# Loading the second chunk of x in halves, moving a weight load ahead of two others, and a new instruction order, in a fused adaLN / linear-attention / SwiGLU kernel

## The chip, the cores and the metric

The kernel runs on one core of a Trainium2 chip. The metric is the device time of one execution in microseconds (us). The kernel before takes about 215 us: 216.03 in the three runs that the prediction had, and medians of 214.80 to 215.99 in the jobs of this study. Executions are compared in the same state. All medians and verdicts below are of fast executions; where a profile fell in the slow state I say so.

## The reference

One transformer block on x of 2048 rows by 512, with modulation from a vector c (`w_mod` gives six vectors of 512):

```python
sa, ca, ga, sb, cb, gb = split(silu(c) @ w_mod)          # six vectors of 512
h = layernorm(x) * (1 + ca) + sa
q, k, v = split(h @ wqkv)                                 # 32 heads of 16
phi = lambda t: concat(softmax(t @ w_phi), softmax(-(t @ w_phi)))   # per head
kv, z = phi(k).T @ v, sum(phi(k))                         # over all 2048 rows
o = (phi(q) @ kv) / (phi(q) @ z + 1e-6)
x = x + ga * (o @ wo)
h = layernorm(x) * (1 + cb) + sb
x = x + gb * ((silu(h @ w_gate) * (h @ w_up)) @ w_down)   # width 1376
```

What matters for the argument: the sum over all rows (`kv`) must be complete before the first attention product can start. The program therefore has a first stage (all keys and values, with the query projections beside it), a hand-over, and a second stage (attention, output projection, feed-forward).

## The kernel before

The program is a list of operations, each with an engine, a planned duration and buffers. A list `ORDER` (one number for an operation, four times its index plus the choice of engine) fixes how they follow each other on each engine. `QUOTA` limits how many PSUM banks each kind of product holds. TensorE therefore works strictly in the listed order: a product that waits for a load stops everything behind it.

All large loads go through SyncE's DMA queue, in this order; `later` and `transposed` put a DMA further back in the same queue:

```python
at_x[0, 0] = load(nc.sync, x_ch[0][:, 0:2, :], ...)       # x in 4 chunks of 512 rows
at_wk = [load(...), load(...)]                             # key weights
at_m1 = [load(nc.sync, wmod_sb[:, k, 0:2 * D], ...) for k in range(KD)]
at_x[0, 1] = load(...)
at_wv = load(...)                                          # value weights
at_x[1] = load(nc.sync, x_ch[1][:], x_v[1], 512)
at_wq = load(nc.sync, wqkv_sb[:, :, 0:D], ...)             # query weights
at_x[2] = load(...)
at_x[3] = load(...)
...
fold_phi(0, Wq2, bWq2, bwq)        # 4 DMA transposes (WT) of the query weights, then 4 products with w_phi
later(wmod_sb[:, :, 2 * D:6 * D], wmod_v[:, :, 2 * D:6 * D])      # second part of w_mod, 2 MB
```

`fold_phi` multiplies the query weights by w_phi once, so that the query projection needs no second product. It needs the weights transposed; for the query weights this is done by DMA, one slice of 128 rows at a time (`WT`).

One tile of 128 rows takes this path in the first stage: a key product (TensorE), two exponentials (ScalarE, `e`), a row sum and a reciprocal (VectorE, `S`, `R`), the product `phik = e * R` (GpSimd, 1.93 us), a copy of the values (`va`), and eight small key-value products of 65 columns that accumulate in PSUM. Four VectorE operations (`KVZ`) read the accumulators at the hand-over.

Fillers are products on a tile of ones, put into planned gaps of TensorE to keep its clock up:

```python
n, each = (4 * (P - HG - 1), 0.108) if not early and not late else (CW, 0.216)
...
fns += [f] * int((o.start - t0 - 0.1) * FILL / each)      # FILL = 0.85 of the gap
```

The softmax here doesn't subtract the row's maximum and nothing guards it: scores larger than these inputs give would overflow.

## Time and profile before

| view of the profile before | value |
|---|---|
| time, median of 3 | 216.03 us |
| span of the profiled execution | 213.2 us |
| TensorE busy | 200.7 us, 94% |
| second part of w_mod: issued, landed | 19.14, 27.32 us |
| TensorE's wait for it | 1.73 us at 27.4 |
| last `phik` on GpSimd ends | 58.6 us |
| first attention product | 61.50 us |

The busy time of TensorE contains fillers, so this document uses the measure that the prediction works out below. **Lag** at a point of the program is the clock time minus the useful product time issued so far. Lag grows when TensorE waits, runs a filler, or runs at half clock. It stays flat where TensorE never waits. Because the useful work is the same in all kernels here, the lags of two kernels at the same useful work say directly which is ahead.

### The profile page before, as it was taken

Reading aid. Unit: us, or ns where it says so; the run is one execution under the profiler, and the core shown is the slowest. Engines: PE = TensorE matmul, PEld = TensorE weight load, DVE = VectorE, ACT = ScalarE, POOL = GpSimd, SP = SyncE. Lnnn points to the kernel's source line nnn. Section 1 sums busy time; section 2 is a strip of 40 time slices with the busy share of each in tenths; the row PEclk is TensorE's granted clock in tenths of the full one; section 3 lists DMA queues with packets and bytes.
Section 4 is the critical chain, followed back from the end, with each engine's and each line's share of the span. In section 5 each row is a group of like instructions: output and inputs, shape, how many; then the busy total and the mean of one; then the engine's idle time right before and its main releaser. Section 6 shows DMA issues by size and latency. Waiting matters only on the chain.

```text
span 213.2 us, 4730 instructions
## 1 busy us (share of the span) xinstructions
PE 200.7 (94%) x1779; PEld 140.2 (66%) x1807; DVE 149.8 (70%) x352; ACT 118.9 (56%) x241; POOL 115.7 (54%) x157
## 2 busy tenths in 40 slices
PE   4997789999999999998999999999999999999993
PEld 1853554555555687786867877777776687777772
DVE  5799969999686977677887596677577764532314
ACT  2677989998889873433533603443342465363230
POOL 5257998899920535672642743654584563441340
PEclk9999999999999999999999999999999999999998
DMA  6996970389600011312221121123211222010001
GB/s 195 363 350 104 389 84 20 71 285 402 217 3 0 0 28 29 74 38 39 54 49 49 39 64 31 46 51 74 52 25 49 51 50 51 28 25 26 28 25 49
DMA packets 30793, 19.24 MB, mean 90 GB/s; under 512 B 22481, under 2 KB 28082, under 8 KB 30770
## 3 DMA queue, kind: packets, MB, share of 16 engines
q1 hardware_dynamic: 30480, 18.85, 31.8%
q8 instruction: 14, 0.23, 0.5%
q10 hardware_dynamic: 290, 0.08, 0.2%
q14 instruction: 9, 0.07, 0.1%
HBM read 11.58 MB, written 2.10 MB: 64 GB/s over the span
## 4 chain that ended last, share of the span: by engine, by line
PE 77%; DMA 13%; SPq 3%; DVE 3%; issue 1%; POOL 1%; DVEq 0%; POOLq 0%
PE one_ps L869 31%; PE one_ps L904 16%; PE one_ps L642 6%; PE one_ps L817 6%; PE one_ps L590 5%; PE one_ps L586 5%; DMA wmod_sb<-in_w_mod_dram 4%; DMA wqkv_sb<-in_A_wqkv_dram 4%; PE four_ps L746 3%; SPq L318 2%; DMA raw<-xn 2%; DMA oT<-o 2%; PE kv_ps L618 2%; DMA wphi_sb<-in_A_w_phi_dram 2%; DVE x_c L820 1%
## 5 line engine op out<-in xcount | busy, mean ns | idle before, releaser
L876 ACT ACTIVATE sg<-one_ps 128x512 bf16<-128x512 f32 (+3 forms) x52 | 27.2, 529 | 44.3 <-PE one_ps L869 39.8
L869 PE MATMUL one_ps<-hT,wu_sb 128*128 128x256 bf16 (+3 forms) x440 | 45.7, 251 | 0.8 <-DVE hT L840 0.8
L869 PE MATMUL one_ps<-hT,wg_sb 128*128 128x256 bf16 (+3 forms) x440 | 44.5, 251 | 0.0
L904 PE MATMUL one_ps<-wd_sb,gu 128*128 128x512 bf16 (+3 forms) x172 | 42.0, 366 | 0.8
L869 PEld LDWEIGHTS <-wu_sb 128*128 128x128 bf16 (+1 forms) x440 | 36.9, 100 | 8.8 <-issue 0.9
L869 PEld LDWEIGHTS <-wg_sb 128*128 128x128 bf16 (+1 forms) x440 | 36.9, 100 | 7.7
L885 POOL TENSOR_TENSOR gu<-usb,sg 128x512 bf16<-128x512 bf16 (+1 forms) x22 | 22.6, 1026 | 22.8 <-ACT sg L876 15.8
L611 POOL TENSOR_TENSOR phik<-e,R 128x1024 bf16<-128x1024 bf16 x16 | 30.6, 1930 | 3.5 <-DVE R L609 2.2
L879 DVE TENSOR_TENSOR gu<-one_ps,sg 128x512 bf16<-128x512 f32 (+2 forms) x30 | 17.8, 595 | 15.9 <-PE one_ps L869 13.0
L904 PEld LDWEIGHTS <-gu 128*128 128x128 bf16 (+1 forms) x187 | 17.8, 98 | 11.9
L375 DVE BATCH_NORM_STATS2 st<-x_c 128x6 f32<-128x512 bf16 x32 | 21.2, 680 | 1.7 <-DMA x_c<-in_A_x_dram 1.4
L883 ACT CAST usb<-one_ps 128x512 bf16<-128x512 f32 (+1 forms) x22 | 11.3, 525 | 18.8 <-PE one_ps L869 15.8
L911 DVE TENSOR_TENSOR fg<-one_ps,gab 128x512 bf16<-128x512 f32 (+1 forms) x17 | 11.2, 656 | 14.8 <-PE one_ps L904 14.5
L804 POOL TENSOR_TENSOR o<-o 128x512 bf16<-128x512 bf16 x14 | 16.2, 1157 | 8.7 <-DVE o L784 8.7
L607 DVE TENSOR_REDUCE S<-e 128x64 f32<-128x1024 bf16 x16 | 19.0, 1194 | 2.2 <-ACT e L597 2.1
L784 DVE TENSOR_TENSOR o<-four_ps,A 128x512 bf16<-128x512 f32 x32 | 20.6, 684 | 0.0
L915 POOL TENSOR_TENSOR ot<-x_c,fg 128x512 bf16<-128x512 bf16 x8 | 9.2, 1154 | 18.5 <-DVE fg L911 18.5
L597 ACT ACTIVATE e<-one_ps 128x512 bf16<-128x512 f32 x32 | 17.3, 607 | 2.7 <-PE one_ps L586 1.7
L648 ACT ACTIVATE eT<-one_ps 128x512 bf16<-128x512 f32 x32 | 17.5, 644 | 1.2 <-PE one_ps L642 1.1
L817 PE MATMUL one_ps<-wo_sb,oT 128*128 128x512 bf16 x60 | 16.2, 379 | 0.5 <-DMA oT<-o 0.3
L820 DVE TENSOR_TENSOR x_c<-x_c,one_ps 128x512 bf16<-128x512 bf16 x16 | 11.0, 687 | 7.5 <-PE one_ps L817 7.2
L590 PE MATMUL one_ps<-wqkv_sb,hT 128*128 128x512 bf16 x62 | 15.8, 379 | 0.1
(102 smaller groups left out, 273.7 us busy)
## 6 DMA issues: line engine op xcount, KB each, us to landing
wmod_sb<-in_w_mod_dram SPq DMA_DIRECT2D x1, 2048.0 KB, 8.2
out_dram<-ot SPq DMA_DIRECT2D x15, 128.0 KB, 1.9
x_c<-in_A_x_dram SPq DMA_DIRECT2D x3, 512.0 KB, 9.4
wg_sb<-in_B_w_gate_dram SPq DMA_DIRECT2D x1, 1376.0 KB, 8.3
wu_sb<-in_B_w_up_dram SPq DMA_DIRECT2D x1, 1376.0 KB, 11.2
wd_sb<-in_B_w_down_dram SPq DMA_DIRECT2D x1, 1280.0 KB, 14.4
wmod_sb<-in_w_mod_dram SPq DMA_DIRECT2D x4, 256.0 KB, 5.0
wqkv_sb<-in_A_wqkv_dram SPq DMA_DIRECT2D x2, 512.0 KB, 7.8
```

What stands on the lines that cost most here:

```text
L375: pl.op("DVE", r=reads, w=[st6], us=0.6, fn=lambda: nc.vector.bn_stats(st6()[:], src))
L590: nc.tensor.matmul(v()[:], lhsT=hT[c_i][k][:, cols], rhs=wqkv_sb[:, k, 2 * D:3 * D], start=(k == 0), stop=(k == KD - 1))
L607: pl.op("DVE", r=[e], w=[Ss], us=1.14, fn=lambda: nc.vector.tensor_reduce(Ss()[:], e()[:].rearrange("p g s h f -> p (g s h) f"), axis=AX.X ...
L611: pl.op("POOL", r=[e, R], w=[bphik[i]], us=1.9, fn=lambda: nc.gpsimd.tensor_tensor(bphik[i]()[:].rearrange("p g s h f -> p (g s h) f"), e( ...
L648: pl.op("ACT", r=[pq, btab], w=[beT[c_i, sg, j]], us=0.48, fn=lambda sg=sg: nc.scalar.activation(eTs[c_i, sg, j][:], pq()[:], ACT.Exp, sca ...
L784: nc.vector.tensor_tensor(o2()[:, sg].rearrange("p j (h d) -> p j h d", d=DH), ndv()[:, :, sg, 0:P].rearrange("p j (h d) -> p j h d", d=DH ...
L817: nc.tensor.matmul(a()[:], lhsT=oT()[:, j, :], rhs=wo_sb[:, j, :], start=(j == 0), stop=(j == KD - 1))
L869: nc.tensor.matmul(ps_()[0:fsz, q * n:(q + 1) * n], lhsT=wt[:, k, m * P:m * P + fsz], rhs=h2[k], start=(k == 0), stop=(k == KD - 1))
L876: pl.op("ACT", r=[g, btab], w=[sg], us=0.08 + 0.41 * L / CW, fn=lambda: nc.scalar.activation(sg()[0:fsz, 0:L], g()[0:fsz, 0:L], ACT.Silu))
L879: pl.op("DVE", r=[u, sg], w=[gu], us=0.07 + 0.535 * L / CW, fn=lambda: nc.vector.tensor_tensor(gu()[0:fsz, 0:L], u()[0:fsz, 0:L], sg()[0:f ...
L885: pl.op("POOL", r=[usb, sg], w=[gu], us=0.05 + 1.06 * L / CW, fn=lambda: nc.gpsimd.tensor_tensor(gu()[0:fsz, 0:L], usb()[0:fsz, 0:L], sg() ...
L904: nc.tensor.matmul(fp()[:], lhsT=b()[0:fsz, c0:c0 + P], rhs=wd_sb[0:fsz, m, cs], start=(m == 0), stop=(m == FM - 1))
```

## The change

Its intent: take away the wait for w_mod by loading it earlier, bring the second chunk of x into the pipeline sooner by normalizing it in halves, start the clock earlier with finer fillers, and lay out the order anew with load times measured on the chip. The diff, cut to its core (`ORDER` is a new list of 952 numbers, not shown):

```diff
-QUOTA = {'q': 3, 'turn': 4, 'T': 2, 'T2': 2, ...}
+QUOTA = {'q': 2, 'turn': 1, 'T': 2, 'T2': 3, ...}
+PAIRS = (0, 1)                                   # chunks whose hT buffers come in halves
 ORDER = [ ... all new ... ]
-    at_x[1] = load(nc.sync, x_ch[1][:], x_v[1], 512)
+    at_x[1, 0] = load(nc.sync, x_ch[1][:, 0:2, :], x_v[1][:, 0:2, :], 256)
+    at_x[1, 1] = load(nc.sync, x_ch[1][:, 2:4, :], x_v[1][:, 2:4, :], 256)
     at_wq = load(nc.sync, wqkv_sb[:, :, 0:D], wqkv_v[:, :, 0:D], 512)
+    at_m2 = [load(nc.sync, wmod_sb[:, :, 2 * D:4 * D], wmod_v[:, :, 2 * D:4 * D], 1024)]
     at_x[2] = load(nc.sync, x_ch[2][:], x_v[2], 512)
+    at_m2.append(load(nc.sync, wmod_sb[:, :, 4 * D:6 * D], wmod_v[:, :, 4 * D:6 * D], 1024))
     at_x[3] = load(nc.sync, x_ch[3][:], x_v[3], 512)
-    later(wmod_sb[:, :, 2 * D:6 * D], wmod_v[:, :, 2 * D:6 * D])
-    first_norm(4, 4)
-    first_T(4, 4)
+    first_norm(4, 2)
+    first_T(4, 2)
+    first_norm(6, 2)
+    first_T(6, 2)
-    n, each = (4 * (P - HG - 1), 0.108) if not early and not late else (CW, 0.216)
+    n, each = (P, 0.056) if early else (CW, 0.216) if late else (4 * (P - HG - 1), 0.108)
-    fns += [f] * int((o.start - t0 - 0.1) * FILL / each)
+    fns += [f] * int((o.start - t0) / each if early else (o.start - t0 - 0.1) * FILL / each)
```

The tile of ones is also set first of all on VectorE, and gate and up weights get separate buffers. Of these two, only the first was part of an experiment (b_fine).

## The prediction

> **What bounds the kernel now.** I read the page's busy shares and slices first, then the chain that ended last, then TensorE's order of time with its waits, and last the busy table by stretches. The busy shares and the row of TensorE's slices:
>
> ```profile
> PE 200.7 (94%) x1779; PEld 140.2 (66%) x1807; DVE 149.8 (70%) x352; ACT 118.9 (56%) x241; POOL 115.7 (54%) x157
> PE   4997789999999999998999999999999999999993
> ```
>
> TensorE is the bound, but "busy" includes filler products on a tile of ones (line L978), which only keep the clock up. So I made a measure of my own. A 512-column product follows its neighbour after 0.216 us where nothing waits (four take 0.86 us in the chain), a 256-column one after 0.109 (16 in 1.75), a 128-column one after 0.056 (8 transposes from 10.03 to 10.49), a 65-column one after 0.032 (24 in 0.77). With these spacings (0.028 for the smallest) all useful products of the program sum to 192.3 us. The clock time less the useful work issued so far I call the lag; some matmul records are missing from the trace, so I counted the work by the program's order and took only the times from the trace. The lag is 8.1 us at 12.5, 10.7 at 18.5, 11.7 at 24.6 and 14.2 at 27.6; then it stays between 14.1 and 14.6 up to 61.5, grows to 15.7 at 76.8, 16.2 at 79.8 and 17.1 at 98.7, and from there to 202.9 it does not move by 0.1: the feed-forward products run at the spacing of an array that never waits. Last products, output and end make up the rest of the 213.2. So the time can fall only before 98.7, and two thirds of the loss is made before 27.6. That piece, in the chain that ended last:
>
> ```profile
> 5.87 7.84 DMA wqkv_sb<-in_A_wqkv_dram
> 13.73 1.44 SPq L318
> 15.22 1.26 SPq L318
> 16.52 1.27 SPq L318
> 17.83 1.27 SPq L318
> 19.14 8.18 DMA wmod_sb<-in_w_mod_dram
> 27.37 0.55 PE one_ps L464 x16
> ```
>
> The query weights land at 13.71; SyncE then issues four transposes at 1.3 us each, and only after them the 2 MB second part of w_mod, which lands at 27.32. TensorE is in program order, so the modulation product stops everything behind it. TensorE's own view just before:
>
> ```profile
> 24.81 0.83 PE L978 MATMUL kv_ps<-ones 128*128 128x252 bf16 x6
> 27.37 0.55 PE L464 MATMUL one_ps<-silucT,wmod_sb 128*128 128x1 bf16 x16 [1.73 <-DMA wmod_sb<-in_w_mod_dram]
> ```
>
> So 0.65 us of filler and 1.73 of idling are that one load. The stretches say what stands behind it (columns: us, then busy us and count of TensorE, weight loads, VectorE, ScalarE, GpSimd, then clock, DMA share, GB/s):
>
> ```profile
> 14.00:20.00 6.00, 4.83 (x31) 2.41 (x31) 6.00 (x15) 4.36 (x9) 4.33 (x5) 1.00 0.84 159
> 20.00:28.00 8.00, 6.15 (x74) 4.21 (x73) 7.94 (x17) 7.97 (x14) 7.27 (x11) 1.00 0.97 295
> 28.00:40.00 12.00, 11.89 (x76) 5.87 (x77) 9.49 (x15) 11.10 (x21) 10.18 (x10) 1.00 0.29 43
> 40.00:60.00 20.00, 19.84 (x187) 10.98 (x189) 16.92 (x27) 17.82 (x35) 18.09 (x11) 1.00 0.75 255
> ```
>
> VectorE is full from 14 to 28, ScalarE from 20 to 28, and ScalarE and GpSimd are near full up to 60. Taking the load's wait away can therefore not give back all it costs.
>
> **What the Trainium skill says.** "Perfetto Trace Analysis", section Identifying the Most-Contended Engine, calls matmul busy share a poor measure of distance to the roof, because of pipelining; the trace agrees: 94% busy, of which useful spacing is 192.3 of 213.2 us, 90%. "TensorE: Matmul & The Clock Gate", section What's actually happening, says the array starts at half clock and is released after about 3.4 us of sustained work. The records print 1.00 throughout, but the spacings agree: the five first fillers stand 0.42 us apart from 3.19, the 128-column products of L512 0.107 apart up to 7.3, and everything after runs at 0.056 and 0.216. "DMA: Bandwidth & Descriptors", section Queues, rings and completion order, says descriptors of a ring are taken in order. The trace agrees for this one SyncE queue: the transposes issued from 13.73 landed at 17.80, 18.38 and 19.01, all after x's last chunk (17.25, issued long before), and those issued at 24.60 landed at 28.60, after w_mod.
>
> **The change part by part.** I read instruction counts and order of both kernels on each engine; durations are those of the trace before.
>
> Start. The tile of ones is now VectorE's first work (0.49 us from 0.78), so fillers start near 1.6 instead of 3.19, and are 128 columns wide: 24 at half clock take 2.6 us and end about when w_phi lands (3.94). Before, five wide ones held TensorE until 5.30, so the block mask product came 1.4 us late, and with it VectorE's first statistics, which stood behind it. But VectorE's new order puts a weight copy (0.6) and three silu steps (0.5) before the second aggregate, which I place at 6.75, against 6.57 to 6.81 before. GpSimd's rstd chain then takes 1.7, two normalizations on VectorE 0.36 each, transposes 0.5, evacuation 1.1: first value product at about 11.4 instead of 11.79. Gain 0.4.
>
> Tiles 2 and 3. VectorE now takes three statistics of chunk 1 (0.68 each) and two normalizations before tile 0's row sums (1.2) and reciprocal (0.5), and only after these half of the evacuation. I get the next key product near 19.1 instead of 18.5. But the first gate product (0.86 us, at 35.5 before) has run in between, as its half of w_mod should land near 16.4: 13.71 plus 1 MB at the 375 to 400 GB/s of the loads before it. Lag 10.4 instead of 10.7: gain 0.3, the earlier 0.4 included.
>
> Chunk 1. The load of w_mod is now ahead of x chunks 2 and 3. By the rate seen in the trace (0.65 us a 256 KB piece, x chunks 1.3 to 1.65), x2 lands near 18, the second half near 20.5 to 21, x3 near 22.3, and the first transposed query weight only after it, near 22.7 to 23, against 17.8 before. The modulation product asks for its data at about 22, so the 2.4 us of filler and idling are gone. The query fold stands near 22.4 and may wait 0.5. Halving chunk 1 means two rstd chains of 1.7 us where there was one of 1.8 (GpSimd +1.6), eight evacuations of 0.5 or 0.36 where there were four of 0.75 or 0.5. ScalarE's order, added up from tile 0's values at 13.0 on with no gap, brings chunk 1's first half of hT to 23.4, tile 3's values to 28.4 (after four normalizations at 0.81), and so the second gate to 28.6: lag 12.1, and 12.3 to 12.5 at 31. Before it was 14.2 to 14.3. Gain 1.9.
>
> The rest up to the turn. From about 25.5 GpSimd owes 15 phi_k at 1.93 us and one rstd chain at 1.9, 30.9 us together, so the last phi_k ends near 56.5 to 57 (58.5 before). Its product stands after 45.8 us of useful work, which allows a lag of 11.2 at best; 12.4 fits. Then four KVZ pieces (2.1 us) have only 1.7 us of query products to hide behind, 0.4 to 0.6 lost; the late fillers (1, 1 and 3 wide ones, before 1, 1 and 1) tell that gaps of about 1.5 us are foreseen before the feed-forward, where the lag grew by 1.1 before (14.6 to 15.7). Loss 0.3.
>
> Feed-forward. Same products in a new order, with other quotas for the transposes' PSUM banks. Before, only two waits cost anything there, 0.5 near 78.5 for a DMA transpose of the attention output and 0.9 near 98 for one of the normalized tile; the rest is at its floor. The new order can save at most these 1.4 and can lose more. The tiles arrive relative to each other as before, so I take 0.6 saved as the middle, with no better ground than that the order was laid out again.
>
> Sum: 1.9 - 0.3 + 0.6 = 2.2 us off 216.0: 213.8.
>
> **The rivals.** (a) All of the removed waiting comes back: chunk 1 lags 9.5 to 10 instead of 14.2, and the time is near 211.5. For it: the fillers before the run of tiles without any sum to 4.1 us against 5.1. Against: VectorE and ScalarE full in 14 to 28. (b) ScalarE and GpSimd simply take the place of the load, or the transposes behind x3 cost 2 us more than the load did: 215.5 to 216. For it: their 89 to 90% in 40 to 60. Against: the new order moves four xn and one hT off GpSimd and four raw hT off ScalarE onto VectorE. (c) The reordering of the last two thirds makes more new waits than the start gains; before it is at its floor from 98.7 on, so a new order can only lose there: 217 to 218. (d) The finer fillers let the array fall back to half clock: a few us. Against: they leave no planned gap.
>
> **Range and chances.** My chain adds about 30 links, each good to 0.1 to 0.2, so 1 us; the feed-forward order adds 0.8 us either way; before's own runs spread 2.2 us. That gives 211.3 to 216.3. Two per cent faster means under 211.7, which needs rival (a) nearly whole: 0.14. Two per cent slower means over 220.3: 0.03. The rest, 0.83, within.
>
> **What would show it.** Right: no wait of the modulation product for w_mod; last x chunk at 22 to 23 and query weights just behind it; ScalarE and VectorE over 95% busy from 14 to 31; first key or value product at 11.2 to 11.6; lag 12 to 13 from 31 to 60 and 15 flat in the feed-forward. Wrong: lag under 11 in that stretch (a), a wait of the query fold of over 1 us or GpSimd without gaps to 59 (b), lag still growing after 100 (c), 128-column products 0.107 apart after 8 us (d).

## The result, and the profile after

The changed kernel takes 221.31 us (median of 4, 221.01 to 221.51) against 215.99 (median of 4) for the kernel before on the same chip. The ratio is 1.0262, with a 95% interval of 1.0203 to 1.0320: slower by 2.6%, outside the predicted range and in the class given a chance of 0.03. A ratio here is the mean time of one kernel's fast runs over that of the other's of the same rounds, so it is not quite the ratio of the medians quoted. The profiled execution is fast, span 219.7 us.

The same rows as before, from the page of the changed kernel (busy shares, then the slices of TensorE and of its granted clock):

```profile
PE 207.6 (94%) x1856; PEld 145.4 (66%) x1856; DVE 152.8 (70%) x364; ACT 118.8 (54%) x236; POOL 112.6 (51%) x157
...
PE   7999399998998999999998999999999999999993
...
PEclk9999969999999999999999999999999999999998
```

TensorE is "busy" for the same share, which says nothing. But slice 5 (about 22 to 27 us) has fallen to 3 tenths, and in slice 6 the granted clock is 6 tenths. The chain that ended last shows what came there:

```profile
6.27 8.64 DMA wqkv_sb<-in_A_wqkv_dram
...
14.98 1.29 SPq L321
...
16.33 3.25 SPq L321
...
19.62 7.03 DMA WT<-wqkv_sb
...
26.70 0.40 PE one_ps L524 x4
...
27.47 3.35 PE one_ps L586 x8
```

The chain no longer passes through w_mod. It passes through a transpose of the query weights, issued at 19.62 and landed at 26.65. TensorE's own order of time at that place (start, us, then the group, and in brackets the idle time before it and what ended that):

```profile
21.96 1.03 PE L590 MATMUL one_ps<-wqkv_sb,hT 128*128 128x512 bf16 x4
22.83 0.34 PE L465 MATMUL one_ps<-silucT,wmod_sb 128*128 128x1 bf16 x8
26.70 0.40 PE L524 MATMUL one_ps<-BD,WT 128*128 128x128 bf16 x4 [3.53 <-DMA WT<-wqkv_sb]
26.93 0.54 PE L465 MATMUL one_ps<-silucT,wmod_sb 128*128 128x1 bf16 x16
27.34 3.48 PE L586 MATMUL one_ps<-Wk,hT 128*128 128x512 bf16 x8
```

Line L465 is the modulation product. It no longer waits for its data: the 1.73 us wait of before is gone, as the change wanted. The product behind it, the first query fold (L524), waits 3.53 us instead. Then eight key products take 3.48 us; where nothing is wrong eight of them take 1.89 (19.76 in the same trace). So the idle time also cost the clock, about 1.6 us more.

The four stretches that the prediction shows of before, here of after (us, then busy us and count of TensorE, weight loads, VectorE, ScalarE, GpSimd, then clock, DMA share, GB/s):

```profile
14.00:20.00 6.00, 6.00 (x62) 4.06 (x61) 4.67 (x14) 5.43 (x11) 3.37 (x6) 1.00 1.04 394
20.00:28.00 8.00, 4.47 (x54) 2.67 (x53) 7.93 (x17) 4.66 (x10) 7.32 (x13) 0.97 1.07 98
28.00:40.00 12.00, 12.00 (x90) 6.29 (x89) 6.74 (x16) 10.99 (x21) 6.11 (x7) 0.88 0.22 44
40.00:60.00 20.00, 19.18 (x147) 9.68 (x146) 18.31 (x27) 18.40 (x36) 17.97 (x10) 1.00 0.73 240
```

From 20 to 28 ScalarE falls from 7.97 to 4.66 us busy: it stood in its own order behind the copy of that query fold. From 28 to 40 GpSimd falls from 10.18 to 6.11, because it gets nothing to multiply. The last `phik` ends at 64.1 instead of 58.6, the first attention product starts at 67.27 instead of 61.50.

The lag by useful work, for both kernels and for the kernels of the experiments, worked out from each profile (us):

| useful work | before | after | a_swap | a_swap_hyb | b_loads | b_pe |
|---|---|---|---|---|---|---|
| 4.6 | 8.1 | 9.2 | 9.2 | 7.9 | 8.7 | 8.5 |
| 10.5 | 10.7 | 11.1 | 11.0 | 10.0 | 17.3 | 10.9 |
| 14.5 | 14.2 | 16.4 | 11.2 | 11.0 | 19.1 | 14.9 |
| 35 | 14.2 | 17.9 | 13.3 | 13.0 | 19.5 | 16.7 |
| 45 | 14.6 | 18.2 | 13.6 | 13.3 | 19.9 | 17.8 |
| 60 | 15.7 | 21.5 | 16.9 | 16.5 | 21.0 | 18.9 |
| 100 | 17.1 | 23.5 | 18.7 | 16.6 | 22.1 | 18.9 |
| 180 | 17.1 | 23.6 | 18.7 | 16.6 | 22.1 | 19.0 |

(The b_loads entry at 10.5 is read at 12, after its wait.) After is level with before up to 10.5, loses 5.3 us by 14.5 (before 3.5), another 5.1 by 60 (before 1.5) and 2.0 by 100 (before 1.4).

### The profile page after: what moved, and what is told of

Read it like the earlier page. It is cut to its first block, busy times and chain, and to the rows that moved or that the text cites. A ratio compares the mean times of both kernels' runs of the same rounds, so it can differ in the third digit from the quotient of the medians.

```text
span 219.7 us, 4868 instructions
## 1 busy us (share of the span) xinstructions
PE 207.6 (94%) x1856; PEld 145.4 (66%) x1856; DVE 152.8 (70%) x364; ACT 118.8 (54%) x236; POOL 112.6 (51%) x157
## 4 chain that ended last, share of the span: by engine, by line
PE 67%; DMA 15%; DVE 5%; POOL 5%; SPq 3%; issue 3%; ACT 1%; DVEq 0%; POOLq 0%; ACTq 0%
PE one_ps L870 30%; PE one_ps L905 14%; PE one_ps L818 5%; DMA raw<-xn 4%; PE one_ps L642 4%; DMA wqkv_sb<-in_A_wqkv_dram 4%; DMA WT<-wqkv_sb 3%; PE one_ps L586 3%; PE four_ps L747 3%; PE one_ps L590 3%; SPq L321 2%; DMA oT<-o 2%; POOL phik L611 2%; DMA wphi_sb<-in_A_w_phi_dram 1%; PE kv_ps L618 1%
## 5 line engine op out<-in xcount | busy, mean ns | idle before, releaser
L870 PE MATMUL one_ps<-hT,wg_sb 128*128 128x256 bf16 (+3 forms) x440 | 45.7, 251 | 0.0
L905 PE MATMUL one_ps<-wd_sb,gu 128*128 128x512 bf16 (+3 forms) x187 | 44.4, 367 | 0.0
L886 POOL TENSOR_TENSOR gu<-usb,sg 128x512 bf16<-128x512 bf16 (+1 forms) x22 | 22.4, 1019 | 31.8 <-ACT sg L877 16.4
L880 DVE TENSOR_TENSOR gu<-one_ps,sg 128x512 bf16<-128x512 f32 (+2 forms) x30 | 17.8, 599 | 18.4 <-PE one_ps L870 13.8
L905 PEld LDWEIGHTS <-gu 128*128 128x128 bf16 (+1 forms) x187 | 17.9, 98 | 12.3 <-DVE gu L880 0.2
L805 POOL TENSOR_TENSOR o<-o 128x512 bf16<-128x512 bf16 x14 | 16.1, 1152 | 15.1 <-DVE o L785 13.7
L884 ACT CAST usb<-one_ps 128x512 bf16<-128x512 f32 (+1 forms) x22 | 11.5, 523 | 17.3 <-PE one_ps L870 15.6
L912 DVE TENSOR_TENSOR fg<-one_ps,gab 128x512 bf16<-128x512 f32 (+1 forms) x17 | 11.2, 658 | 13.0 <-PE one_ps L905 12.8
L648 ACT ACTIVATE eT<-one_ps 128x512 bf16<-128x512 f32 x32 | 17.8, 605 | 2.8 <-PE one_ps L642 2.6
L597 ACT ACTIVATE e<-one_ps 128x512 bf16<-128x512 f32 x32 | 17.3, 606 | 1.6 <-POOL phik L611 1.3
L818 PE MATMUL one_ps<-wo_sb,oT 128*128 128x512 bf16 x64 | 16.4, 379 | 1.3 <-DMA oT<-o 1.3
L586 PE MATMUL one_ps<-Wk,hT 128*128 128x512 bf16 x64 | 17.0, 409 | 0.6 <-DVE hT L555 0.6
L590 PE MATMUL one_ps<-wqkv_sb,hT 128*128 128x512 bf16 x64 | 16.5, 394 | 0.0
L405 ACT ACTIVATE xn<-x_c,ln_nmr,ln_rstd 128x512 bf16<-128x512 bf16 x17 | 13.6, 822 | 4.3 <-POOL ln_nmr L390 4.3
```

The source lines that it names most:

```text
L586: nc.tensor.matmul(pk()[:], lhsT=hT[c_i][k][:, cols], rhs=Wk2[:, k, :], start=(k == 0), stop=(k == KD - 1))
L590: nc.tensor.matmul(v()[:], lhsT=hT[c_i][k][:, cols], rhs=wqkv_sb[:, k, 2 * D:3 * D], start=(k == 0), stop=(k == KD - 1))
L648: pl.op("ACT", r=[pq, btab], w=[beT[c_i, sg, j]], us=0.48, fn=lambda sg=sg: nc.scalar.activation(eTs[c_i, sg, j][:], pq()[:], ACT.Exp, sca ...
L818: nc.tensor.matmul(a()[:], lhsT=oT()[:, j, :], rhs=wo_sb[:, j, :], start=(j == 0), stop=(j == KD - 1))
L870: nc.tensor.matmul(ps_()[0:fsz, q * n:(q + 1) * n], lhsT=wt[:, k, m * P:m * P + fsz], rhs=h2[k], start=(k == 0), stop=(k == KD - 1))
L886: pl.op("POOL", r=[usb, sg], w=[gu], us=0.05 + 1.06 * L / CW, fn=lambda: nc.gpsimd.tensor_tensor(gu()[0:fsz, 0:L], usb()[0:fsz, 0:L], sg() ...
```

## The experiments

Eighteen kernels ran, in five jobs; all gave correct results. The names: `a_` starts from the changed kernel, `b_` from the kernel before, `hyb` from the repaired kernel a_swap_hyb.

### First job: the load order, the transposes, the fillers

**a_swap** takes the changed kernel and issues the four transposes in the order in which TensorE's folds want them. The first fold in TensorE's order uses the third slice.

```diff
-                transposed(lambda cols=cols: WTb[:, :, cols], lambda i=i: wqkv_sb[:, i, 0:D], [bw[i]], [part])
+                u = (2, 0, 1, 3)[i]
+                transposed(lambda u=u: WTb[:, :, u * P:(u + 1) * P], lambda u=u: wqkv_sb[:, u, 0:D], [bw[i]], [part])
```

> The changed kernel with one difference: the four transposes of the query weights are issued on the SyncE queue in the order third, first, second, fourth slice, so that the slice whose fold stands first in TensorE's order is also the first to land (23.35 us in the changed kernel's trace) instead of the third (26.65). Theory W (the wait for that slice, and what hangs on it, is the main loss): the 3.5 us wait falls to about 0.3, the array keeps full clock at 27 to 31 (1.6 us), ScalarE's copy of the fold no longer stands 3.3 us in front of the later work; lag at 31 us about 11.5 to 12.5 instead of 16.4, and 215 to 217.5 us. Rival O (the new order of everything after the start is slower by itself): the lag at 31 falls by 5 but comes back by the turn, 219 to 221 us. Rival F (the engines behind, VectorE and GpSimd, bound the first third): lag at 31 falls by less than 2, 219.5 us or more.

Measured: 217.01 us (13 runs), ratio 1.0070 [1.0045, 1.0095]. From 1.0262 that is 1.9%, 4.1 us, won by changing one statement. TensorE's order of time at the same place:

```profile
22.75 0.34 PE L465 MATMUL one_ps<-silucT,wmod_sb 128*128 128x1 bf16 x8
23.25 0.40 PE L525 MATMUL one_ps<-BD,WT 128*128 128x128 bf16 x4 [0.15 <-ACT hT L428]
23.48 0.54 PE L465 MATMUL one_ps<-silucT,wmod_sb 128*128 128x1 bf16 x16
23.88 1.89 PE L587 MATMUL one_ps<-Wk,hT 128*128 128x512 bf16 x8
```

The fold waits 0.15 us instead of 3.53, and the key products run at full clock. The lag at 14.5 is 11.2, even 3 us below the kernel before. So the wait was the main cost of the changed kernel. But a_swap is still slower than before: its lag grows from 11.2 to 18.7, that of before from 14.2 to 17.1.

**b_loads** takes the kernel before and makes only the new load order: w_mod's second part in two halves, ahead of x chunks 2 and 3.

```diff
+    nc.sync.dma_start(wmod_sb[:, :, 2 * D:4 * D], wmod_v[:, :, 2 * D:4 * D])
     at_x[2] = load(nc.sync, x_ch[2][:], x_v[2], 512)
+    nc.sync.dma_start(wmod_sb[:, :, 4 * D:6 * D], wmod_v[:, :, 4 * D:6 * D])
     at_x[3] = load(nc.sync, x_ch[3][:], x_v[3], 512)
-    later(wmod_sb[:, :, 2 * D:6 * D], wmod_v[:, :, 2 * D:6 * D])
+    pl.op("XBAR", r=[bsp], w=[bsp], us=0.5, fn=lambda: None)
```

> The kernel before with the loads of the change only: the second part of w_mod in two halves of 1 MB, one ahead of x chunk 2 and one ahead of x chunk 3, and none after the transposes; order and fillers as before. Theory W: the transposed query weights land at about 23.3 instead of 17.8, in ring order behind the loads, while the order asks for them at 17.8; TensorE waits about 5 us there, the clock falls to half, and the 1.7 us wait for w_mod at 27 is gone; net 2 to 5 us slower than before, 218 to 221 us. Rival: the wait for w_mod was the worse one and the fold's wait is hidden: 214 to 216 us.

Measured: 220.10 us (4 runs), ratio 1.0223 [1.0157, 1.0289].

```profile
16.50 0.81 PE L980 MATMUL kv_ps<-ones 128*128 128x512 bf16 x3
22.69 0.61 PE L525 MATMUL one_ps<-BD,WT 128*128 128x128 bf16 x4 [5.39 <-DMA WT<-wqkv_sb]
```

In the old order the fold stands even earlier, and waits 5.39 us. The load order by itself, without any new instruction order, makes the kernel slower by 2.2%: moving 2 MB ahead in a queue moves everything behind it back.

**a_wide** gives the changed kernel the old filler rule, and **b_fine** gives the kernel before the new one.

```diff
 a_wide:
-        n, each = (P, 0.056) if early else (CW, 0.216) if late else (4 * (P - HG - 1), 0.108)
+        n, each = (CW, 0.216) if early or late else (4 * (P - HG - 1), 0.108)
-        fns += [f] * int((o.start - t0) / each if early else (o.start - t0 - 0.1) * FILL / each)
+        fns += [f] * int((o.start - t0 - 0.1) * FILL / each)
 b_fine: the reverse in the kernel before, with the tile of ones set first
```

> The changed kernel with the filler rule of the kernel before in the start: 512 columns each, 85% of each planned gap, 10 of them instead of 73 of 128 columns; everything else as in the changed kernel. The changed kernel's 128-column products stood 0.107 us apart up to 13.8 us, the kernel before's only up to 7.3. Theory: it is the width of the fillers and the gaps between that keep the array at half clock; then full clock comes by 8 us, the first eight products of tile 0 and 1 take 1.73 instead of 2.57 us, lag at 15 about 8.4 instead of 9.2, and the time falls by 0 to 1 us, since the wait for the query weights absorbs it. Rival: the release of the clock depends on where dense work falls and the start's real products are themselves too sparse; half clock lasts to 12 us or later with wide ones too, and the time is within 0.5 us of the changed kernel or worse.

> The kernel before with the fillers of the change only: the tile of ones made first, 128 columns each, no gap left in the plan; loads and order as before. If finer fillers by themselves keep the array at half clock, the first eight products (at 11.8 us in before) take over 2.5 us instead of 1.74 and the time is 0.5 to 1.5 us longer. If the new order's sparser start does it, full clock comes by 8 us here and the time is the same or up to 0.8 us shorter, as the mask product no longer stands behind five wide fillers.

Measured: a_wide 218.84 us (4 runs), ratio 1.0159 [1.0102, 1.0217]; b_fine 217.53 us (4 runs), ratio 1.0104 [1.0042, 1.0166]. Both at first look say that fine fillers cost about 1%. The traces show this only at a remove. In a_wide's trace the query weights landed at 13.57 instead of 14.90, and the third transposed slice at 25.18 instead of 26.65. In b_fine the first products come no later than before, and the loss stands after the wait for w_mod, which was 2.12 us instead of 1.73 and dropped the clock:

```profile
28.15 0.55 PE L462 MATMUL one_ps<-silucT,wmod_sb 128*128 128x1 bf16 x16 [2.12 <-DMA wmod_sb<-in_w_mod_dram]
28.56 1.02 PE L588 MATMUL one_ps<-wqkv_sb,hT 128*128 128x512 bf16 x4
29.42 3.15 PE L584 MATMUL one_ps<-Wk,hT 128*128 128x512 bf16 x8
```

So these two left the fillers open; the next job settles it for the repaired kernel. One difference goes with the early fillers in every trace of this study: in all eight kernels with wide ones the query weights land at 13.50 to 14.22 us, in all twelve with fine ones at 14.27 to 15.45 (b_fine: 14.77, and its w_mod is therefore issued at 20.04 instead of 19.14). Fine fillers are more instructions, and a 16 KB transfer that the profile lists as "instruction", some 1.1 us on one DMA engine, starts at 11.6 to 12.9 us with them, while the weights are still landing, and at 13.7 to 15.1 us with the wide ones. In the changed kernel a second one starts at 24.54, among the transposes; in a_wide there is none of that size between 16 and 32 us. No run tests whether these transfers are the cause of the later landings.

### Second job: the new late order, the fillers again, another place for w_mod

**a_swap_hyb** is a_swap with the order and the two bank quotas of the kernel before from the hand-over on (operations 324 and up; their indices are 4 higher than in the kernel before). **a_swap_wide_hyb** has the old filler rule as well. **b_late** is the reverse: the kernel before with the late order and quotas of the changed one.

```diff
 a_swap_hyb:
-QUOTA = {'q': 2, 'turn': 1, 'T': 2, 'T2': 3, ...}
+QUOTA = {'q': 2, 'turn': 4, 'T': 2, 'T2': 2, ...}
+ORDER: every entry of an operation >= 324 replaced, place by place, by the next such entry of the kernel before, plus 16
 a_swap_wide_hyb: a_swap_hyb and the edit of a_wide
 b_late: the kernel before, entries of operations >= 320 from the changed kernel, minus 16; 'turn': 1, 'T2': 3; 'q': 3 kept
```

> The changed kernel with the transposes issued in slice order 2,0,1,3 (as a_swap) and, from the hand-over of the PSUM banks on (attention, output projection, feed-forward), the order and bank quotas of the kernel before. Theory (the new late order itself costs): a_swap grew its lag from 13.6 to 18.7 us between useful work 45 and 100, the kernel before from 14.6 to 17.1; with the old late order it should grow by 2.5 from 13.6 to about 16.1, so about 214.4 us, 2.6 below a_swap. Rival (a_swap only meets later what a stage that runs ahead always meets, data or engines that are not ready earlier): within 0.6 us of a_swap's 217.0, lag again about 18.5 at useful 100.

> As a_swap_hyb, and the early fillers as in the kernel before (512 columns wide, 85% of the gap). Theory: the finer fillers at the start cost 0.9 us (lag at useful work 4.6: 9.24 against 8.30 in a_wide) and that carries through, so about 213.5 us, 0.9 below a_swap_hyb. Rival: the start is absorbed by the waits for w_mod and the transposes behind it, then within 0.3 us of a_swap_hyb.

> The kernel before with only the late order and the bank quotas of the changed kernel (from the hand-over of the PSUM banks on). Theory (the new late order itself costs): lag from 14.6 at useful work 45 to about 19.5 at 100, so about 218 us, ratio 1.011. Rival (it costs nothing by itself): lag 17.1 at 100 and 215.3 to 216 us.

Measured: a_swap_hyb 214.61 us (12 runs), ratio 0.9978 [0.9956, 0.9999]. The old late order and its bank quotas (not tested apart) win 0.9%, 2.0 us, and with them the changed kernel is level with the kernel before or a little ahead. Up to useful work 60 the two differ by 0.3 us of lag, at 100 by 2.1: 16.6 against 18.7. In a_swap the output projection (L819) waits twice for DMA transposes of the attention output; this line of its waits (us in total, times, longest) has no counterpart in a_swap_hyb:

```profile
PEld L819 <- DMA oT<-o: 1.5, 2, 1.2
```

So the new late order does cost in the repaired kernel. b_late took 216.42 us (10 runs), ratio 1.0049 [1.0010, 1.0087]: the same sign, but about 1.1 us instead of 2.0. In its profile most of the loss is not even the order: the wait for w_mod was 2.08 us and dropped the clock, which cost 1.7 us of lag before the late order begins. From useful work 45 to 100 its lag grows 3.2 us, where that of the kernel before grows 2.5. So b_late confirms the cost only weakly; that the late order costs less where TensorE arrives later is a guess.

a_swap_wide_hyb took 215.51 us (20 runs), ratio 1.0015 [1.0002, 1.0029]: wide fillers are 0.8 us slower here, not 0.9 us faster. My reading of the first job falls: in the repaired kernel the finer fillers do not make the time longer. (b_fine stays 1.0% slower than the kernel before; that fine fillers cost something where TensorE waits for the query weights, or for what is issued behind them, is not ruled out.) What I took for their effect at the start, half clock up to about 13.8 us, comes and goes with the same instructions. Here is the value product at the start, first of after, then of a_swap_hyb, whose programs are the same up to that point:

```profile
12.11 2.74 PE L590 MATMUL one_ps<-wqkv_sb,hT 128*128 128x512 bf16 x8
```

```profile
11.65 1.89 PE L591 MATMUL one_ps<-wqkv_sb,hT 128*128 128x512 bf16 x8 [0.35 <-DMA wqkv_sb<-in_A_wqkv_dram]
```

**b_m2act26** puts the second part of w_mod of the kernel before on ScalarE's DMA queue, so that the transposes don't stand behind it in SyncE's.

```diff
         def evac(act):
+            if kind == "T" and w == 4 and jp == 0:
+                nc.scalar.dma_start(wmod_sb[:, :, 2 * D:6 * D], wmod_v[:, :, 2 * D:6 * D])
-    later(wmod_sb[:, :, 2 * D:6 * D], wmod_v[:, :, 2 * D:6 * D])
+    pl.op("XBAR", r=[bsp], w=[bsp], us=0.5, fn=lambda: None)
```

> The kernel before with the second part of w_mod issued on ScalarE's DMA queue at the modulation of the second chunk (about 16 us), not on SyncE's behind the transposes (19.14 us). Theory (what the change wanted, w_mod there in time, can be had without delaying the transposes behind it in the same queue): w_mod lands near 23 to 24 instead of 27.3, the 1.73 us wait at 27.4 goes, the lag at useful work 14.5 is 12.3 to 12.8 instead of 14.2; if it carries to the end 213.5 to 214.3 us. Rival: the two queues share the same engines, the transposes land later (over 22 us) and the query folds wait instead: 215 to 218 us.

Measured: 222.35 us (4 runs), ratio 1.0348 [1.0315, 1.0382]. The experiment missed its aim: I hung the load on the wrong modulation, it was issued at 24.82 us and landed at 33.33. It shows only how much a late w_mod costs: a wait of 7.3 us and half clock behind it.

### Third job: what eats the lead?

a_swap_hyb is 3.2 us ahead at useful work 14.5 and 0.5 ahead at the end. In its trace the last `phik` ends at 59.1, no earlier than in the kernel before (58.6), and the last seven follow each other without a gap. My theory was that GpSimd's chain bounds the first stage, and that a lead of TensorE is worth nothing there.

**hyb_R** moves one reciprocal on VectorE ahead of three modulations (GpSimd had waited 1.97 us for it). **hyb_pe** adds 24 fillers on TensorE, **hyb_pool** eight small additions on GpSimd, 2.6 and 2.5 us. **b_m2act16** is b_m2act26 with the load at the right modulation.

```diff
 hyb_R: ORDER: entry 1020 (a reciprocal R) moved from behind 972 to behind 1016
 hyb_pe, in kv_tile:
+            for q in range(3 if 4 <= i < 12 else 0):
+                nc.tensor.matmul(<free columns of kv_ps>, lhsT=ones, rhs=ones, start=False, stop=True)   # 252 columns
 hyb_pool, behind phik:
+            if 4 <= i < 12:
+                nc.gpsimd.tensor_scalar_add(junk[:], mhalf[:], 0.0)
 b_m2act16:
-            if kind == "T" and w == 4 and jp == 0:
+            if kind == "T" and w == 2 and col0 == 2 * P and jp == 0:
```

> a_swap_hyb with one VectorE instruction moved: the reciprocal of the key sums of one tile (the one that GpSimd waited 1.97 us for at 45.8) stands ahead of the three modulations that wait for the transposes of x. Theory (GpSimd's chain of 16 phi_k products of 1.93 us sets when attention can start, not TensorE): the last phi_k ends 1.2 to 1.6 us earlier than 59.1, the first attention product starts near 61 instead of 62.34, and the time falls by 0.8 to 1.5 us from 214.6 to 213.1 to 213.8. Rival (TensorE's own order sets it, GpSimd's wait is slack): within 0.3 us of a_swap_hyb.

> a_swap_hyb with 24 more filler products of 252 columns on TensorE, three behind each of the key-value products of tiles 4 to 11 (24 x 0.109 = 2.6 us of TensorE's time between 31 and 54 us). If TensorE bounds the key and value stage: 2.6 us longer, 217.2. If GpSimd's chain bounds it (with VectorE and ScalarE in front of it): at most 0.8 us longer.

> a_swap_hyb with 8 small additions on GpSimd, one behind each phi_k of tiles 4 to 11 (0.23 us each at a spacing of 0.31, 2.5 us in all). If GpSimd's chain bounds the key and value stage: 1.5 to 2.5 us longer (its 1.97 us wait may take up some), 216.1 to 217.1. If TensorE bounds it: at most 0.5 us longer.

> The kernel before with the second part of w_mod issued on ScalarE's queue at about 15.5 us (b_m2act26 placed it at the wrong modulation, 24.8 us). It should land at 22 to 24 us and the 1.73 us wait at 27.4 go, with the transposes of the query weights up to 2 us later. If TensorE's lag at 28 us carries to the end: 1.2 to 2 us faster than before, 213.3 to 214.1. If the key and value stage is bound by GpSimd, the wait was hidden: within 0.6 us of before, 214.7 to 215.8.

Measured: hyb_R 216.08 us (22 runs), ratio 1.0086 [1.0062, 1.0111], 2.3 us slower than a_swap_hyb where I expected it faster (its runs fall in two groups, 13 at 215.5 to 216.3 and 9 at 217.2 to 218.1; the lower one alone is slower than every run of a_swap_hyb). hyb_pe 217.73 us (4 runs), ratio 1.0115 [1.0056, 1.0174]. hyb_pool 215.08 us (12 runs), ratio 1.0001 [0.9973, 1.0028], 0.5 us slower. The theory falls: 2.5 us more on GpSimd cost 0.5 (up to 1.3 within the intervals), where it asked for 1.5 to 2.5, and a reciprocal sooner for GpSimd cost time. The trace of hyb_R shows why: the modulated tile now came later to TensorE's key product, and GpSimd then waited 3.07 us for the exponentials of that product.

```profile
47.66 1.04 PE L587 MATMUL one_ps<-Wk,hT 128*128 128x512 bf16 x4 [1.96 <-DVE hT L556]
```

b_m2act16: 218.50 us (the three fast ones of four runs), ratio 1.0149 [1.0075, 1.0224]; its profile fell in the slow state, so I use only landings and the wait from it. The load was issued at 14.87 on ScalarE's queue and landed at 25.33, but the first transpose, issued at 13.90 on SyncE's, landed only at 22.42 (17.80 in the kernel before), and the fold waited 5.47 us. A queue of its own did not help: the first transpose landed 4.6 us later all the same, though nothing new stood ahead of it in its own queue. The likely reason is that the two queues share the DMA engines.

### Fourth job: which engine has room?

**hyb_act** adds five copies on ScalarE (2.5 us), **hyb_dve** five reciprocals on VectorE (2.3 us), **b_pe** gives the kernel before the fillers of hyb_pe. **hyb_xn** moves two of the four normalizations of chunk 3 from ScalarE to VectorE.

```diff
 hyb_act, behind the exponentials:
+            if i in (4, 6, 7, 9, 10):
+                nc.scalar.copy(junk[:], ones[:, 0:256])
 hyb_dve, behind the reciprocal R:
+            if i in (4, 6, 7, 9, 10):
+                nc.vector.reciprocal(junk[:], Ss()[:])
 hyb_xn: ORDER: 625 and 633 (ScalarE) taken out, 624 and 632 (VectorE) put behind 656
 b_pe: the edit of hyb_pe in the kernel before
```

> a_swap_hyb with five more 256-column copies on ScalarE, behind the exponentials of key tiles 4, 6, 7, 9 and 10 (5 x 0.51 = 2.5 us). If ScalarE, busy 12.00 of 12 us between 28 and 40, is what keeps the stage from running ahead: 1.8 to 2.5 us longer than a_swap_hyb (216.4 to 217.1, ratio to before 1.006 to 1.010). If not: under 0.7 us longer.

> a_swap_hyb with five more 64-column reciprocals on VectorE, behind the reciprocals of the same tiles (5 x 0.46 = 2.3 us). If VectorE (11.15 of 12 us between 28 and 40) is what holds: 1.6 to 2.3 us longer. If not: under 0.7 us longer.

> a_swap_hyb with two of chunk 3's four normalizations moved from ScalarE (0.85 us each, the last at 39.65) to VectorE (0.31 us each, near 34.7). If chunk 3's chain (normalization, transposes, which landed last at 44.0, modulation, key product) bounds the stage: the last transpose lands 1.2 to 1.8 us earlier, VectorE's 0.75 us wait for it goes, the last phi_k ends 0.7 to 1.5 us earlier and the time is 0.6 to 1.3 us below a_swap_hyb (ratio to before 0.992 to 0.995). If the bound is elsewhere: within 0.3 us of a_swap_hyb, or slower by the 0.6 us that VectorE has more.

> The kernel before with the 24 more filler products of hyb_pe (2.6 us of TensorE between 31 and 54 us). If TensorE bounds that stage in the kernel before, as its flat lag (14.1 to 14.6 us from 28 to 61) suggests: 2.3 to 2.6 us longer, ratio 1.011 to 1.012. If the other engines set its pace: under 1 us longer.

Measured, beside those of the third job (cost is the ratio less that of a_swap_hyb, or less 1 for b_pe, times 215; first attention product from the profile, 62.34 in a_swap_hyb, 61.50 before; the last column is the difference in lag ahead of the added work, which is the scatter of the start):

| kernel | work added | time, ratio | cost, us | first attention product later by | of it already at useful work 13.5 |
|---|---|---|---|---|---|
| hyb_pe | TensorE 2.6 us | 217.73, 1.0115 | 2.9 | 1.46 | 0.2 |
| hyb_pool | GpSimd 2.5 us | 215.08, 1.0001 | 0.5 | 1.37 | 0.7 |
| hyb_act | ScalarE 2.5 us | 215.47, 1.0008 | 0.6 | 1.59 | 0.7 |
| hyb_dve | VectorE 2.3 us | 216.06, 1.0030 | 1.1 | 1.17 | 0.2 |
| b_pe | TensorE 2.6 us, kernel before | 216.60, 1.0081 | 1.7 | 3.22 | 0.7 |

(The delays come from one execution each. The intervals of the ratios make each cost good to 0.5 to 0.8 us, that of hyb_pe to 1.3: the costs of hyb_pool and hyb_act are not clear of nothing.)

How full the engines of a_swap_hyb are after the start (columns as in the stretches above):

```profile
28.00:40.00 12.00, 11.80 (x101) 6.41 (x100) 11.15 (x19) 12.00 (x23) 9.82 (x9) 1.00 0.27 54
40.00:50.00 10.00, 9.40 (x65) 4.52 (x64) 8.68 (x14) 9.03 (x18) 7.94 (x6) 1.00 0.78 265
```

In the kernel before, the added TensorE work appears in full at the first attention product (3.22 us, less the 0.7 of a longer wait for w_mod in that execution): TensorE bounds its first stage. Part is given back later, since the old second stage loses less when it starts late (lag from 17.8 at useful work 45 to 18.9 at 100, before 14.6 to 17.1). In a_swap_hyb, work added to any one of the four engines delays the first attention product, by 0.7 to 1.3 us once the scatter of the start is taken off: three to five tenths of its size. No engine alone is the bound. All four are so nearly full (79 to 100% in the two stretches) that each seems to pass a part of its delay on to the others. hyb_pe's 2.9 us at the end is more than its delay at the hand-over: its profile shows 0.8 us and 1.2 us lost later on (near 93 and 163 us), with only four runs behind the median, so I do not read it as more than "TensorE counts most".

hyb_xn took 216.18 us (22 runs), ratio 1.0026 [1.0007, 1.0045]: 1.0 us slower, not faster. The chain of chunk 3 is not the bound by itself either. The two normalizations took 2.15 us on VectorE, not 0.62: the first ran 1.83 us while GpSimd was at a `phik` (34.97 to 36.90). The Trainium skill has the rule that I had overlooked ("SBUF — State Buffer", section Who interferes with whom): VectorE and GpSimd share a pair of ports, and where VectorE's instruction runs in a mode that uses both, the one that comes second is blocked for the whole of the other; the trace agrees: the first normalization began behind that `phik`, the second, after its end, took 0.40 us. The reciprocal behind them came late, GpSimd's next product with it (1.70 us of waiting), and TensorE waited 1.49 us for that:

```profile
35.22 2.15 DVE L401 TENSOR_SCALAR xn<-x_c,ln_rstd,ln_nmr 128x512 bf16<-128x512 bf16 x2
```

```profile
40.58 0.43 PE L619 MATMUL kv_ps<-va,phik 128*128 128x65 bf16 x8 [1.49 <-POOL phik L612]
```

### Fifth job: the hand-over

In the trace of a_swap_hyb three steps between the last key-value product and the first attention product cost 1.1 us of lag. The kernel before loses nothing there, because other products stand in that place:

```profile
59.24 0.43 PE L619 MATMUL kv_ps<-va,phik 128*128 128x65 bf16 x8
59.51 1.02 PE L643 MATMUL one_ps<-hT,Wq 128*128 128x512 bf16 x4
60.82 0.27 PE L971 MATMUL kv_ps<-ones 128*128 128x252 bf16 x1 [0.29 <-DVE KVZ L718]
60.93 1.03 PE L643 MATMUL one_ps<-hT,Wq 128*128 128x512 bf16 x4
62.34 0.66 PE L748 MATMUL four_ps<-KVZ,eT 128*128 128x144 bf16 x8 [0.38 <-DVE KVZ L718]
```

The third line is a filler that itself waits: it writes the accumulators that VectorE is still reading. **hyb_nofill** leaves it out; **hyb_rot** also moves each later query group one place forward.

```diff
 hyb_nofill:
-        if late and not o.news:
+        if late and not o.news or not late and o.start > kv_ops[-1].start:
             return
 hyb_rot: hyb_nofill, 'q': 3, and in ORDER the query groups 804, 840, 1220, 1208, 1056, 1232, 828
          each at the place of the one before it, the first ahead of 1300 (the first attention product)
```

> a_swap_hyb without the one filler product behind the last key-value product, which waited 0.29 us (0.45 us of lag, and 0.11 of its own) for VectorE's read of the accumulators. If the first attention product waits for that read anyway: nothing, 214.3 to 214.8 us as a_swap_hyb, and the 0.38 us wait before the first attention product grows to about 0.9. If the filler's wait was a loss of its own: 0.4 to 0.5 us less.

> hyb_nofill with one more query group (4 products, 0.86 us) between the last key-value product and the first attention product, and each later query group one place forward. If the hand-over only lacks work to fill the wait for the accumulators: the first attention product starts at about 62.4 as before but with 0.86 us more useful work done, and 0.5 to 0.9 us is won, 213.7 to 214.1, ratio to before 0.993 to 0.996. If the work is only missing further on, where the last of the moved groups stood: within 0.3 us of a_swap_hyb.

Measured: hyb_nofill 214.25 us (20 runs), ratio 0.9945 [0.9925, 0.9966]; hyb_rot 214.73 us (22 runs), ratio 0.9985 [0.9968, 1.0002]. Without the filler the kernel is the fastest of this study, 0.55% below the kernel before, which is still within 2%. Against a_swap_hyb the gain is 0.7 us by the ratios, but the two intervals overlap (they are of different jobs), so I call it likely. In hyb_nofill's profile the wait before the first attention product is 0.59 us. Filling that wait (hyb_rot) did not win more: the moved work was then missing further on. In its trace the first attention product waits for nothing, but ten wide fillers stand between 66 and 76 us, where a_swap_hyb has six.

## Why the prediction was wrong

The prediction said 213.8 us; the time is 221.3. By its own steps:

**The wait for w_mod.** Right. The two halves landed at 17.61 and 21.56 (predicted 16.4 and 20.5 to 21), x's last chunk at 22.87 (22.3), and the modulation product did not wait. Landings were predicted to about one us.

**The query fold. This is the step that failed.** The prediction said: "The query fold stands near 22.4 and may wait 0.5." Its place was 0.8 us out: TensorE came to it at about 23.2. The first transposed slice was also near enough, 23.35 against 22.7 to 23. But TensorE's new order takes the third transposed slice first, and that one was issued third and landed at 26.65. I had compared the fold's place with the landing of the first transpose, without looking up which slice the fold reads. Nor did the slices follow each other as before: the third landed 3.3 us behind the first, against 1.2 (17.80 to 19.01) in the kernel before; at that spacing the wait would have been about 1.4 us (my estimate from these landings). The wait was 3.53 us instead of 0.5, and the idle time dropped the clock, 1.6 us more, which the sum had no term for. a_swap shows it by one changed statement: 4.1 us. It also shows that the rest of this step was right or even pessimistic: with the slices in order the lag at 14.5 is 11.2, where the prediction had 12.1 to 12.5.

**The feed-forward and the late order. The second step that failed.** The prediction took 0.6 us saved "with no better ground than that the order was laid out again". a_swap_hyb shows that the new late order costs 2.0 us. This was rival (c), which I had named with the right argument (an order at its floor can only lose) and given no weight in the sum. It did not show as I said it would, by lag still growing after 100: the lag is flat at 23.5 from there. The loss stands between 60 and 100, where a_swap gains 1.8 us of lag and a_swap_hyb none.

**The rest up to the turn.** Predicted loss 0.3 from 12.4. Measured in a_swap_hyb from 11.0 at 14.5 to 16.5 at 60, where the kernel before goes from 14.2 to 15.7: about 4 us more growth, so the whole lead of 3.2 us and all of the predicted 1.9 goes here. About half of it goes up to useful work 45, in the first stage (2.3 us of growth against 0.4), and half between 45 and 60, at the hand-over and behind it (3.2 against 1.1). (Half a us of lead comes back by 100, since the kernel before loses 1.4 us there and a_swap_hyb nothing.) For the first half the fourth job gives the reason: from 28 us on, all four engines of the first stage are nearly full, so TensorE cannot keep a lead. In the second half 1.1 us are the hand-over of the fifth job, for which the prediction had 0.4 to 0.6; behind it a_swap_hyb's trace has six wide fillers between 65 and 75 us, the kernel before three, and no experiment took that apart. The first half was rival (b) in part ("ScalarE and GpSimd simply take the place of the load"). It is not GpSimd or ScalarE alone. The prediction saw the full engines in the stretches, wrote that the wait "can therefore not give back all it costs", and then let nearly all of the gain through.

**The start.** Predicted gain 0.4, first value product at 11.4. In after it came at 12.11 and at half clock, at 11.65 and full clock in a_swap_hyb with the same program. Rival (d) was visible in after's trace (128-column products 0.107 apart at 10 us) but it was not an effect of the fillers (with wide ones the same eight products took 2.61 us in a_wide, 2.74 in after), and by 10.5 us of useful work it had shrunk to 0.4 us of lag behind the kernel before, probably because waits for data take it up.

**The sum.** In ratios: the order of the transposes 1.9% (4.1 us), the late order 0.9% (2.0 us), and what is left, 0.2% better than before (0.5 us), is what the load order, the halves and the early order are worth together. 4.1 + 2.0 - 0.5 = 5.6 us slower, as measured (2.6% of 216); by the intervals of the ratios the 4.1 is good to about 1.4 and the 2.0 to about 0.7. What stays open: why b_late and a_swap see different costs of the late order, and whether the early fillers are what delays the query weights.

**The range.** It was built from link errors of 0.1 to 0.2 us each. Such a range has no room for a single wait of several us that was looked for in the wrong place. A chance of 0.03 for "slower" was too small for a change that puts 2 MB ahead of four small transfers on which TensorE's order depends.

## What to carry to other kernels

When a load moves ahead in a queue, list everything behind it, with the landing that each consumer in the engine's order needs, by slice and not by tile: a transfer of 2 MB ahead of four small ones costs more than its own wait did if the first consumer wants the third. When an order is laid out anew, change it only in the part that the change needs; the old order of the untouched part, with its bank quotas, was worth 2 us here. A lead won early can be lost in the next stage in which every engine is nearly full, and adding a known amount of work to one engine at a time shows quickly which stage that is.

## What the Trainium skill lacked or had wrong

- "TensorE: Matmul & The Clock Gate", section What's actually happening: release to full clock after about 3.4 us of sustained work. Here products ran from 1.44 us with short gaps, and the same program was at full clock by about 9.8 us in one trace (a_swap_hyb) and still at half clock at 12.11 us in another (after, eight 512-column products in 2.74 us instead of 1.89). The page's half a us of variation is for back-to-back products; for a start with gaps, as here, these traces differ by over 2 us.
- The same page, in its rules for kernels (section Why this matters for your kernels), asks for gaps under about 3 us. Here a gap of 2.08 us (b_late) and one of 2.12 us (b_fine) were each followed by half clock 1.5 to 1.7 us after their end, lasting some 3 us, while one of 2.21 us (b_pe) and one of 1.73 us (before) were not. So a gap of about 2 us was already too long in two of these four traces, and harmless in the other two.
- "DMA: Bandwidth & Descriptors", section Queues, rings and completion order: in-order consumption within a ring agrees (the first transpose, issued at 14.98, landed behind x's last chunk at 22.87). What I found on no page is how long this can hold the issuing engine: issuing the second transpose took 3.25 us instead of 1.3 (at 16.33 in after, with the loads still pending), and held back the two behind it. The runs do not show what it waited for.
